# A transformer layer on one core: V from gathered columns in all nine units, one PSUM tile for each part of the last pair, and new engine orders

## The chip, the core and the metric

The kernel runs on one core of a Trainium2 chip. The core has five engines that run side by side, each through its own list of instructions: TensorE (PE, matrix products; its weight loads are shown as PEld), VectorE (DVE), ScalarE (ACT), GpSimd (POOL) and SyncE (SP), which here only issues DMAs. ScalarE issues some DMAs too. Engines wait for each other through semaphores. The metric is the device time of one execution in microseconds, the median of several runs.

## The reference

The input x has 2048 rows (tokens) of 448 numbers in bf16. A small vector c gives six modulation vectors. The layer has an attention half and a feed-forward half:

```python
mod = silu(c) @ w_mod                      # 6 x 448: sa, ca, ga, sb, cb, gb
h = layernorm(x) * (1 + ca) + sa
qkv = h @ wqkv                             # 16 heads of 28
# token s attends to tokens s, s-2, s-4, ..., s-14 (8 keys, where they exist)
logits = q . k * 28 ** -0.5
o = softmax(logits) @ v
x = x + ga * (o @ wo)
h = layernorm(x) * (1 + cb) + sb
x = x + gb * (silu(h @ w1) @ w2)           # hidden size 1792
```

Since keys lie two tokens apart, even and odd tokens never meet in the attention.

## The kernel before

**Tiles.** The 2048 tokens are split by parity into two series of 1024. A *pair* m (0 to 7) is 128 positions of both parities, 256 tokens, two tiles of 128 rows. A *chunk* k (0 to 3) is two pairs. The normalised and modulated activations lie transposed, features on the partitions, in two tiles `hA` and `hB` of 512 positions each (shown as ha and hb), as [feature, parity, block, position]. The 448 features lie in four blocks of 128, so that a product over 448 is seven matmuls of 64 rows. Two of these, on the upper and lower 64 rows, run side by side. Each such product is two operations: S, four steps on equal halves, and C, three steps on crossed halves (function `pair`). C starts only after S has ended, so other work is put between them.

**Stages.** For every chunk: statistics (L361, L362), `rstd` on GpSimd (L374, L375), the shift `nm` on VectorE or GpSimd (L381, L383, L385), the normalised `xn` on ScalarE (L393) or VectorE (L395). The first chunk is transposed by TensorE (L455) and modulated out of PSUM in blocks (`modp`, L234 on ScalarE, L236 on VectorE); the other chunks are transposed by DMA (L412) and modulated in place (`mod`). The Q and K weights are copied to a padded tile `wp` (`pad`, L441). Then come the Q and K products (L483), evicted at L487.

**Attention units.** Queries are handled in nine units u of two blocks of 57 positions, each block with its 64 keys. `project_v(u)` computes V for a unit's keys, both blocks and both parities. A key block of 64 positions starts anywhere, and its two parities lie 512 columns apart or more, so there are two ways to feed it as stationary operand. *Apart*: two matmuls of 64 rows by 64 columns, one for each parity, four running side by side, 28 in all (L518). *Whole*: the columns are first copied (`gather`, L507) to a tile `hv`, where both parities lie next to each other, and then 14 matmuls of 64 by 128 do it (L517). A set says which units are apart; all but unit 4 are, whose keys lie across hA and hB. After V come logits (L555), exp on ScalarE (L562), the mask (L613), the weighted sum of V (L629), reciprocal and scaling (L636, L641), a transpose by DMA (L644), the copy to its place (`align`, L651 to L659), and the output projection (L686) with the residual (L694).

**Feed-forward.** For each chunk: 14 column blocks of w1 in seven products (L714), silu on ScalarE (L719), and for each pair the product with w2 (L741), an addition of x on VectorE (`ya`, L774) and a store (`sto`, L779). The last pair, m = 7, is done in pieces so that its end is short: `full` (L753) computes F0 and F1 (rows of parity 0), F2 (parity 1, first 224 columns) and F3 (parity 1, last 224 columns), with three additions ya70, ya71, ya72 and three stores (L781). All four write one PSUM tile.

**Order.** Each of the 578 operations has a number and an engine; `ORDER` lists them, and `Plan.emit` issues them in that order, so that it is every engine's program. The letter behind a number chooses the engine (p TensorE, a ScalarE, v VectorE, g GpSimd, s SyncE). There are four PSUM tiles of two banks; an operation with `take=("ps",)` takes the next free one, and `P.release` says which operation gives it back. Where two engines write overlapping parts of a tile, the framework adds a wait for the one issued first. TensorE fills its first microseconds with products of zeros (`warm_up`, L297): "warm" is 12 matmuls, and each "junk" two; a junk given to SyncE is nothing. Should a sum of exponentials fall out of range, the layer runs again in a safe form (L891); this doesn't happen with these inputs.

## Time and profile before

| | us |
|---|---|
| median of 3 runs | 170.31 |
| lowest, highest | 169.68, 170.35 |
| the profiled execution | 169.34 |
| its span, first to last instruction | 167.5 |
| TensorE busy | 156.1 |
| ScalarE busy | 102.0 |
| VectorE busy | 86.1 |
| GpSimd busy | 25.5 |

A row of the profile in order of time has the start in us from the span's start, the length in us, the engine (SPq and ACTq: a DMA being issued), the line of the kernel, the operation, out<-in by tile names, the shape, and how many instructions were merged; in brackets stands the engine's idle time before it and what ended it. A row of the grouped view has the line, engine, operation, tiles and count, then busy us, mean ns of one, and idle us before. A row of DMA issues has tiles, issuing queue, count, size, and us from issue to landing. Matmuls overlap, so the length of one (349 or 376 ns) is longer than the distance from one to the next; a stretch of many is read from the start of its first to the start of what follows.

### The profile page before, as it was taken

Reading aid. Unit: us, or ns where it says so; the run is one execution under the profiler, and the core shown is the slowest. Engines: PE = TensorE matmul, PEld = TensorE weight load, DVE = VectorE, ACT = ScalarE, POOL = GpSimd, SP = SyncE. Lnnn points to the kernel's source line nnn. Section 1 sums busy time; section 2 is a strip of 40 time slices with the busy share of each in tenths; the row PEclk is TensorE's granted clock in tenths of the full one; section 3 lists DMA queues with packets and bytes.
Section 4 is the critical chain, followed back from the end, with each engine's and each line's share of the span. In section 5 each row is a group of like instructions: output and inputs, shape, how many; then the busy total and the mean of one; then the engine's idle time right before and its main releaser. Section 6 shows DMA issues by size and latency. Waiting matters only on the chain. (4 is left out here: it accounts for less than half of the span.)

```text
span 167.5 us, 6069 instructions
## 1 busy us (share of the span) xinstructions
PE 156.1 (93%) x2670; PEld 80.5 (48%) x2670; DVE 86.1 (51%) x192; ACT 102.0 (61%) x138; POOL 25.5 (15%) x66
## 2 busy tenths in 40 slices
PE   2979979999999999999999999999999999999950
PEld 1254535655455555444556444454444444445540
DVE  3897899987888747692668713302152002002220
ACT  4368657879866869997976695894266620440000
POOL 7460730700002200312034000022000000000000
PEclk9999999999999999999999999999999999999996
DMA  5989978658640999920220950002411000000412
GB/s 138 348 293 242 247 289 135 180 101 171 162 126 21 198 174 293 250 56 7 59 66 22 121 125 4 0 0 57 126 55 55 4 0 4 0 0 4 170 32 87
DMA packets 33453, 18.52 MB, mean 111 GB/s; under 512 B 25102, under 2 KB 33422, under 8 KB 33422
## 3 DMA queue, kind: packets, MB, share of 16 engines
q1 hardware_dynamic: 30208, 14.46, 37.6%
q10 hardware_dynamic: 3214, 3.61, 6.9%
q8 instruction: 23, 0.38, 0.9%
q14 instruction: 8, 0.07, 0.1%
HBM read 10.21 MB, written 1.84 MB: 72 GB/s over the span
## 5 line engine op out<-in xcount | busy, mean ns | idle before, releaser
L719 ACT ACTIVATE both<-ps 128x1024 bf16<-128x1024 f32 x28 | 27.8, 1021 | 23.6 <-PE ps L714 23.6
L741 PE MATMUL ps<-w,both 64*128 64x448 bf16 x392 | 39.9, 349 | 0.0
L714 PEld LDWEIGHTS <-w 64*128 64x128 bf16 x392 | 19.0, 94 | 21.9
L741 PEld LDWEIGHTS <-both 64*128 64x128 bf16 x392 | 18.8, 94 | 18.2
L714 PE MATMUL ps<-wqk,w 64*128 64x512 bf16 x196 | 23.3, 376 | 0.0
L714 PE MATMUL ps<-h,w 64*128 64x512 bf16 x196 | 23.1, 376 | 0.0
L562 ACT ACTIVATE p<-ps 128x912 bf16<-128x912 f32 x18 | 15.8, 928 | 5.7 <-PE ps L555 5.6
L483 PEld LDWEIGHTS <-wp 64*128 64x128 bf16 x224 | 11.0, 94 | 13.4 <-issue 3.2
L694 DVE SCALAR_TENSOR_TENSOR x_all<-ps,x_all 128x448 bf16<-128x448 f32 x16 | 9.3, 621 | 15.0 <-PE ps L686 15.0
L483 PE MATMUL ps<-ha,wp 64*128 64x512 bf16 x112 | 13.2, 377 | 1.1 <-DVE ha L236 1.1
L483 PE MATMUL ps<-hb,wp 64*128 64x512 bf16 x112 | 14.0, 377 | 0.0
L487 ACT CAST qk<-ps 128x1024 bf16<-128x1024 f32 x11 | 11.0, 1016 | 4.0 <-PE ps L483 4.0
L374 POOL TENSOR_SCALAR rs<-mv 128x2 f32<-128x2 f32 x16 | 3.9, 242 | 61.3 <-ACT scr L371 45.6
L393 ACT ACTIVATE xn<-x_all,nm,rs 128x512 bf16<-128x512 bf16 x12 | 9.1, 806 | 6.2 <-DVE nm L381 5.7
L613 DVE TENSOR_TENSOR p<-p,maskb 128x1824 bf16<-128x1824 bf16 x9 | 10.1, 1118 | 4.4 <-ACT p L562 4.4
L774 DVE TENSOR_TENSOR wqk<-ps,x_all 128x896 bf16<-128x896 f32 x4 | 4.4, 1089 | 15.5 <-PE ps L741 13.4
L375 POOL TENSOR_TENSOR rs<-rs,negh 128x2 f32<-128x2 f32 x16 | 11.8, 740 | 1.3
L774 DVE TENSOR_TENSOR ot<-ps,x_all 128x896 bf16<-128x896 f32 x3 | 3.3, 1091 | 16.1 <-PE ps L741 16.1
L361 DVE BATCH_NORM_STATS2 st<-x_all 128x6 f32<-128x448 bf16 x16 | 9.7, 605 | 3.3 <-DMA x_all<-in_A_x_dram 3.3
L395 DVE TENSOR_SCALAR xn<-x_all,mv,rs 128x512 bf16<-128x512 bf16 x20 | 7.3, 402 | 6.9 <-POOL rs L375 6.5
L371 ACT ACTIVATE scr<-x_all,mv 128x448 bf16<-128x448 bf16 x16 | 10.6, 665 | 0.1
L641 DVE TENSOR_TENSOR o<-ps,rc 121x896 bf16<-121x896 f32 x9 | 9.7, 1078 | 0.2
(96 smaller groups left out, 170.8 us busy)
## 6 DMA issues: line engine op xcount, KB each, us to landing
both<-in_w_mod_dram SPq DMA_DIRECT2D x3, 672.0 KB, 6.0
w<-in_B_w_dram SPq DMA_DIRECT2D x3, 448.0 KB, 4.4
x_all<-in_A_x_dram ACTq DMA_DIRECT2D x2, 448.0 KB, 4.7
out_dram<-wqk SPq DMA_DIRECT2D x4, 224.0 KB, 2.0
w<-in_B_w_dram ACTq DMA_DIRECT2D x1, 784.0 KB, 6.1
w<-in_B_w_dram SPq DMA_DIRECT2D x1, 784.0 KB, 5.7
both<-in_w_mod_dram SPq DMA_DIRECT2D x3, 224.0 KB, 5.1
wo<-in_A_wo_dram ACTq DMA_DIRECT2D x1, 672.0 KB, 5.0
```

Source lines behind the costliest of these rows:

```text
L361: V.bn_stats(out=st[:], in_=x_all[:, us[t], :])
L371: S.activation(out=scr[:, t, :], in_=x_all[:, us[t], :], func=ACTF.Square, bias=mv[:, t, 0:1], accum_out=mv[:, t, 1:2])
L375: G.tensor_tensor(out=rs[:], in0=rs[:], in1=negh[:], op=ALU.pow)
L483: return [matmul(t[:, j, :], lhsT=w, rhs=hT[k // 2][rows, :, kt, CP * (k % 2):CP * (k % 2) + CP], start=start, stop=stop)]
L487: copy_on(o)(out=qk[:, :, g, :, s0:s0 + CP], in_=t[:].rearrange("p j (t s) -> p j t s", t=2))
L562: S.activation(out=p_of[u][:, 2 * t * w:2 * t * w + 2 * w].rearrange("p (j n) -> p j n", j=2), in_=bank(a, t)[:, :, 0:w], func=ACTF.Exp, s ...
L613: V.tensor_tensor(out=p, in0=p, in1=m, op=ALU.mult)
L641: V.tensor_tensor(out=dims(t[0:n, :], 0, (576, 2), (DH, H), (1, DH)), in0=view(bank(a))[:, :, :, 0:DH], in1=r, op=ALU.mult)
L694: V.scalar_tensor_tensor(out=x_all[:, u, :], in0=ps[first["slot"]["ps"][0]][:, par, 0:D], scalar=1.0, in1=x_all[:, u, :], op0=ALU.mult, op ...
L714: return [matmul(t[:, i // 7, :], lhsT=w1[rows, kt, 128 * i:128 * i + 128], rhs=h[rows, :, kt, :], start=start, stop=stop)]
L719: S.activation(out=hid[:, k % 2, :, i, :], in_=t[:], func=ACTF.Silu)
L741: x = matmul(t[:, par, 0:D], lhsT=hid[half(hf), k % 2, jj, ii, 128 * j:128 * j + 128], rhs=w2[half(hf), ii + 7 * jj, :], start=(way == 0 a ...
```

## The change

Three things change.

1. `APART` becomes empty: all nine V units are "whole". Eight more gathers are issued, and 8 x 28 matmuls of 64x64 become 8 x 14 of 64x128. A gather reads the modulated activations of all pairs that hold its keys.
2. The last pair takes three PSUM tiles: one for F0 and F1, one for F2, one for F3. Each addition reads its own, and each tile is given back by its own addition.
3. `ORDER` is another list, of 586 operations. Its numbers are not comparable with the old ones, since the eight gathers shift them. By name, the parts of it that differ at the start and the end are these (junks on SyncE left out):

| engine | before, start | after, start |
|---|---|---|
| SyncE | ldx0a ldx0b ldm_a1 ldx1 ldm_a0 ldwv0 ldwqk0, n13.tr n12.tr, ldm_b0 ldm_c0 ldm_c1 ldm_b1, n14.tr ldwo1 n15.tr | ldx0a ldc ldx0b ldx1 ldm_a0 ldwqk1 ldwqk0 ldwv0 ldwv1, n13.tr ldm_c1 n12.tr, ldm_b0 ldw21 ldwo0, n15.tr ldm_b1 n14.tr |
| GpSimd | vone3 rcone masks, rstd of n10, n11, n13, vone2, n13.nm, n12.rstd, vone1, n12.nm, vone0, rstd of n15, n14, ones ozero0 ozero1 | ozero1 vone3 masks vone2 vone1 ones, n10.rstd n10.nm n11.rstd n11.nm n12.rstd n13.rstd n13.nm n14.rstd vone0 rcone n15.rstd n15.nm ozero0 |
| ScalarE | ldc tab silu_c scT, n10.xn0 ldwv1 n10.xn1 n11.xn0 ldwqk1 n11.xn1, h00.mod1, ldx2 ldx3, n13.xn0 n13.xn1, pad2, v0.ev v1.ev qk02.ev qk03.ev | tab ldm_a1 silu_c, n10.xn0 scT n10.xn1 ldx2 n11.xn0 n11.xn1 ldx3, h00.mod1 h01.mod0, n12.xn0 n12.xn1, hv0 hv1, qk01.ev qk00.ev qk03.ev |
| VectorE | statistics and shifts of the first four tiles, mod1.ev, h00.mod0 h01.mod0 h01.mod1, pad0, n12.xn0 n12.xn1 screp, pad3 pad1 | statistics of the first four tiles, mod1.ev, pad2 pad3, h00.mod0 h01.mod1, pad0 pad1, n12.nm n13.xn0 n13.xn1 |
| TensorE | ccol warm, 6 junks, mod1.mm h00.trp h01.trp, v0.S v1.S v0.C v1.C, qk03 and qk02, qk01 and qk00, qk11 and qk10 with lg0 between | ccol warm, 3 junks, mod1.mm h00.trp h01.trp, 5 junks, qk00 and qk01, qk02 and qk03, v1.S v0.S lg0 v0.C v1.C, qk10.S qk13.S lg1 |

Here n1m is pair m's normalisation (st, rstd, nm, xn, tr), ldx the loads of x, ldm those of w_mod, ldwqk, ldwv, ldwo, ldw1, ldw2 those of the weights, hv a gather, ozero and vone and rcone and ones memsets of constant parts, `.ev` an eviction. At the end, before: F0 F1 F2 F3, then ya6, ya70, sto70 (SyncE), ya71, sto71 (SyncE), sto6 (SyncE), ya72, sto72 (ScalarE). After: ya6, sto6 (SyncE), F0 F1 F2, ya70, sto70 (ScalarE), ya71, sto71 (ScalarE), F3, ya72, sto72 (SyncE). Between these, every engine's list is another, too: the gathers of units 0, 1, 2 and 5 are on ScalarE, the others on VectorE.

```diff
-APART = (0, 1, 2, 3, 5, 6, 7, 8)
+APART = ()
...
 ORDER = """
-2a 25a 58a 59p 60a 0s 30g 33g 68v 69v 1s 26g 70g 74v 75v 76g 71v 4s 35p 54p 72a 6a 73a 39p 51s 37p 44p 42p 50p 40s 41s 9s 52s 53s 43s 3s 111v 110v
...
-374s 514s 562p 563p 564p 567p 568p 569p 570p 571p 565v 572v 573s 574v 575s 566s 576v 577a
+32g 0s 68v 30g 25a 26g 4a 69v 2s 58a 59p 29g 28g 34g 35p 57p 39p 45s 46p 70g 71g 72a 60a 73a 42s 1s 75v 74v 76g 77g 9s 3s 52s 8s 7s 62p 106v 107v 10a
...
+557a 510p 511p 567p 568p 569p 512p 570p 513v 514s 522s 571p 572p 573v 574s 575p 576p 577p 578p 580v 581a 582v 583a 579p 584v 585s
 """
...
             if last_pair:
-                def full(o, par, i0, i1, c0, c1, i=i, cell=cell):
-                    t = ps[cell["first"]["slot"]["ps"][0]]
+                def full(o, par, i0, i1, c0, c1, i=i, mms=mms):
+                    t = ps[mms[2 * par + (c0 > 0)]["slot"]["ps"][0]][:, 0, 0:c1 - c0]
                     for ii in range(i0, i1):
                         for jj in range(2):
-                            matmul(t[:, par, c0:c1], lhsT=hid[:, k % 2, jj, ii, 128 * (2 * i + par):128 * (2 * i + par) + 128], rhs=w2[:, ii + 7 * jj, c0:c1],
+                            matmul(t, lhsT=hid[:, k % 2, jj, ii, 128 * (2 * i + par):128 * (2 * i + par) + 128], rhs=w2[:, ii + 7 * jj, c0:c1],
                                    start=(ii == 0 and jj == 0), stop=(ii == 6 and jj == 1))
...
-                                  take=() if x else ("ps",), group=("F", None, 0))
+                                  take=() if x == 1 else ("ps",), group=("F", None, 0))
...
-                V.tensor_tensor(out=t[:, p, c0:c1], in0=ps[cell["first"]["slot"]["ps"][0]][:, p, c0:c1], in1=x_all[:, 2 * m + p.start:2 * m + p.stop, c0:c1], op=ALU.add)
+                r = ps[(mms[2 * par + (c0 > 0)] if last_pair else cell["first"])["slot"]["ps"][0]]
+                r = r[:, p, :][:, :, c0:c1] if par is None else r[:, 0:1, 0:c1 - c0]
+                V.tensor_tensor(out=t[:, p, c0:c1], in0=r, in1=x_all[:, 2 * m + p.start:2 * m + p.stop, c0:c1], op=ALU.add)
...
-            P.release(ad, first, "ps")
-            if not last_pair:
+            P.release(ad[:1], first, "ps")
+            if last_pair:
+                for x in (1, 2):
+                    P.release(ad[x:x + 1], mms[x + 1], "ps")
+            else:
                 P.release(st, ad[0], "out")
```

## The prediction

> **What bounds the kernel now.** I read the page first, then TensorE alone in order of time, then the other engines in the two stretches where TensorE waits: the first 22 us and the last 6.

> ```profile
> span 167.5 us, 6069 instructions
> PE 156.1 (93%) x2670; PEld 80.5 (48%) x2670; DVE 86.1 (51%) x192; ACT 102.0 (61%) x138; POOL 25.5 (15%) x66
> PE   2979979999999999999999999999999999999950
> ```

> The profiled execution took 169.34 us, of which 167.5 are the span and 1.84 lie around it. TensorE is full in every slice but the first few and the last two. So a change counts in three ways only: when the unbroken stream of matmuls starts, how much work is in it, and what follows its end. TensorE in order of time:

> ```profile
> 3.22 5.03 PE L297 MATMUL ps<-junk 64*128 64x512 bf16 x24
> 8.90 0.95 PE L322 MATMUL ps<-scT,both 128*128 128x1 bf16 x32 [0.65 <-DMA both<-in_w_mod_dram]
> 9.71 1.05 PE L455 MATMUL ps<-ident,xn 128*128 128x128 bf16 x16
> 10.83 0.70 PE L518 MATMUL ps<-wv,ha 64*64 64x448 bf16 x8
> 11.80 2.73 PE L518 MATMUL ps<-wv,ha 64*64 64x448 bf16 x48 [0.27 <-ACT ha L234]
> 14.47 6.54 PE L483 MATMUL ps<-ha,wp 64*128 64x512 bf16 x58
> 21.36 0.39 PE L483 MATMUL ps<-ha,wp 64*128 64x512 bf16 x2 [0.36 <-DVE ha L236]
> 22.45 1.47 PE L483 MATMUL ps<-ha,wp 64*128 64x512 bf16 x12 [0.70 <-DVE ha L236]
> ...
> 31.20 1.52 PE L518 MATMUL ps<-wv,ha 64*64 64x448 bf16 x28
> 32.55 0.70 PE L629 MATMUL ps<-v,p 64*57 64x29 bf16 x64
> ...
> 39.33 0.94 PE L517 MATMUL ps<-wv,hv 64*128 64x448 bf16 x8
> 40.20 0.70 PE L555 MATMUL ps<-qk 28*64 28x57 bf16 x64
> 40.83 0.74 PE L517 MATMUL ps<-wv,hv 64*128 64x448 bf16 x6
> ```

> The stream begins with V of units 0 and 1 (L518), ragged until 11.80 because the activations arrive piece by piece. The first Q/K product (L483) starts at 14.47. It stands still for 0.36 and 0.70 us at 21 to 22.45, and from there nothing stops it until the last product.

> **The tail.** The rows after the last product (L753):

> ```profile
> 155.75 5.51 PE L753 MATMUL ps<-w,both 128*128 128x448 bf16 x42
> 156.47 1.09 DVE L774 TENSOR_TENSOR wqk<-ps,x_all 128x896 bf16<-128x896 f32 x1 [2.06 <-DMA out_dram<-wqk]
> 161.36 1.22 DVE L774 TENSOR_TENSOR qk<-ps,x_all 128x448 bf16<-128x448 f32 x3 [3.80 <-PEq L891]
> 162.01 1.17 SPq L781 DMA_DIRECT2D out_dram<-qk  x2
> 162.61 0.38 ACTq L781 DMA_DIRECT2D out_dram<-qk  x1
> 163.24 0.42 SPq L779 DMA_DIRECT2D out_dram<-wqk  x1
> ```

> ```profile
> out_dram<-wqk SPq DMA_DIRECT2D x1, 224.0 KB, 2.4
> out_dram<-qk SPq DMA_DIRECT2D x1, 56.0 KB, 2.0
> L774 DVE TENSOR_TENSOR qk<-ps,x_all 128x224 bf16<-128x224 f32 x2 | 0.7, 379 | 0.0
> ```

> All three additions of the last pair run after the last matmul (155.75 + 5.51 = 161.26), although the first has had its sum for some 3 us: all four groups write one PSUM tile. Then SyncE issues two of the three stores and, only behind them, the store of pair 6, whose addition was done at 157.56. That store lands last, at 163.24 + 2.4 = 165.64, and 1.86 us later the span ends. So 6.24 us follow the last matmul.

> After the change, addition one and two each wait for their own PSUM tile and fall under the matmuls that remain; their stores go to ScalarE's queue, where nothing else waits. Pair 6's store goes out ahead of the last one on SyncE. What is left behind the last matmul is 0.10 (161.36 - 161.26) + 0.38 for one addition of 224 columns + 0.03 to the issue (162.61 after the addition's end at 162.58) + 2.0 landing + 1.86 = 4.37 us. Gain 6.24 - 4.37 = **1.87 us**. Bounds: 1.0 if the additions still wait for the last matmul (161.26 + 0.10 + 1.22 + 0.03 + 2.0 + 1.86 = 166.47 against 167.5), 2.3 if a quarter of the final 1.86 us runs beside the landing. Covers: 2.8 us of matmuls hide the first addition's 0.63, some 1.2 the second's 0.38.

> **The V units.** 28 matmuls of 64x64 occupy TensorE from 31.20 to 32.55: 1.35 us. The 14 gathered ones of 64x128 take 0.87 (39.33 to 40.20) and up to 0.74, 1.6 at most, but in two pieces with other shapes of matmul between, which the 1.35 hasn't.  I take nothing for TensorE; bounds -0.4 (shared shapes saved elsewhere) to +0.8 for eight units (0.1 us each, 0.05 a piece). The eight added gathers are two copies of 128x512 each, four on VectorE and four on ScalarE (unit 4's was on VectorE already):

> ```profile
> L507 DVE COPY hv<-ha 128x504 bf16<-128x504 bf16 x1 | 0.3, 287 | 0.0
> L651 ACT COPY oa<-op 128x448 bf16<-128x448 bf16 x1 | 0.6, 564 | 0.9 <-DMA op<-o 0.9
> ```

> That is 0.6 us a unit on VectorE and 1.2 on ScalarE, some 2.3 and 4.8 us in all, on engines busy 51 and 61% of the span. They hide under TensorE's stream as long as no eviction queued behind them is late; the first, on ScalarE ahead of the first Q/K evictions, have 6 us of Q/K products over them.

> **The start.** Gathered V needs all of the first chunk and its copies, so now Q/K goes first, and it cannot begin on a part: it needs both pairs' eight modulated blocks and all four padded weights. The rows that time this:

> ```profile
> 6.51 0.81 ACT L393 ACTIVATE xn<-x_all,nm,rs 128x512 bf16<-128x512 bf16 x1 [3.02 <-DVE nm L381]
> 9.40 0.80 ACT L393 ACTIVATE xn<-x_all,nm,rs 128x512 bf16<-128x512 bf16 x1
> 11.19 0.56 ACT L234 ACTIVATE ha<-ps,modc 128x256 bf16<-128x256 bf16 x1 [0.98 <-DVE ha L236]
> 11.65 0.56 ACT L234 ACTIVATE ha<-ps,modc 128x256 bf16<-128x256 bf16 x1
> ...
> 10.36 2.00 DVE L236 TENSOR_SCALAR ha<-ps,modc 128x256 bf16<-128x256 bf16 x6
> 13.56 0.69 DVE L441 COPY wp<-wqk 128x896 bf16<-128x896 bf16 x2
> 19.82 2.58 DVE L236 TENSOR_SCALAR ha<-ha,modc 128x512 bf16<-128x512 bf16 x3
> ...
> 4.12 0.29 POOL L279 TENSOR_SCALAR_AFFINE_SELECT maskb<-maskb 64x114 bf16<-64x114 bf16 x1
> 5.16 0.19 POOL L374 TENSOR_SCALAR rs<-mv 128x2 f32<-128x2 f32 x1 [0.75 <-DVE mv L362]
> 10.05 0.22 POOL L385 TENSOR_SCALAR nm<-nm 128x2 f32<-128x2 f32 x1
> 19.40 0.10 POOL L286 MEMSET onesf<- 128x1 f32 x1
> 19.99 2.26 POOL L283 MEMSET o<- 128x1088 bf16 x2
> ```

> GpSimd first. Its masks ended at 4.41 and the first rstd began at 5.16, when its statistics came. Now one memset of ob (half of 2.26: 1.13), two more V memsets (0.35) and the ones (19.40 to 19.99: 0.6) stand ahead of it, and rc's memset (0.3) moves away: it begins at about 4.41 + 1.8 = 6.2, 1.0 late. The shift nm, formerly VectorE's, follows on GpSimd, 0.5. So ScalarE's first normalisation begins at about 7.6 instead of 6.51. The other three follow at 0.8 each, with scT between, and end near 10.9 instead of 10.20. The second pair's eight transposes (half of 1.05) end near 11.5.

> VectorE: padding two, 0.7; pair 0's two blocks at 0.33 (2.00 / 6) to 11.7; pair 1's two to 12.4; padding two more to 13.1. The half of the Q and K weights that the old order loaded last was padded at 13.56; now some 0.9 MB fewer stand ahead of it in the queues (V's weights and the other half), so I take both halves as early enough. ScalarE's blocks each wait for VectorE's of the same pair, as at 11.19; two take 1.02 us, so four run from 11.75 to 13.7. TensorE can take up its first pair of matmuls near 13.2 and is free near 13.7: I take **13.5**.

> In the old order, V0 and V1 back to back would be 14 groups at 0.19 (1.35 / 7), 2.65 us, so the stream effectively began at 14.47 - 2.65 = 11.8. Slip **+1.7**; bounds +0.8 (GpSimd's list costs nothing) and +2.5 (weights or clock a microsecond later).

> Against it stand the two stalls, 0.36 + 0.70 = **-1.06**. They came from VectorE's three blocks of 19.82, 2.58 us for what takes 1.1 elsewhere, while GpSimd ran its two memsets of 19.99. In the new order one memset is done at the start, and the second chunk's blocks are needed only near 23.3: 13.5 + 28 pairs at 0.225 (6.54 / 29) + 2 x 1.4 for V0 and V1 + 0.70 for a unit's logits. [...]

> Later in the stream, third-chunk blocks have hardly any slack in the new order: VectorE's list puts pair 4's normalisation behind the masks of units 0 and 1. I add **+0.3** for new stalls; bounds 0 and 1.5.

> **Sum.** 169.34 - 1.87 + 1.7 - 1.06 + 0 + 0.3 = 168.4 in a profiled execution. The median of the runs is 170.31, 0.97 above the profiled one, so I predict **169.3 us**, 0.6% less. About 0.5%, 0.85 us, is what a measurement of this kernel can tell from no change.

> **The rivals.**

> *The start slips little.* If GpSimd's list fits ahead of the statistics, the slip is 0.8 and no new stall comes: 169.3 - 0.9 - 0.3 = 168.1. For it: TensorE's five fillers behind the transposes fill only 5 x 0.23 = 1.1 us, too little for 2 us. Against: the memsets' durations above. Chance 0.20.

> *A slow clock, slower than before.*

> ```profile
> L297 PE MATMUL ps<-junk x24: 377/627/631, 3.2 to 7.9; 64*128 64x512 bf16 x24
> ```

> The fillers run at 0.42 us a pair (5.03 / 12); only the last, at 7.9, has the 377 ns of the later products, which go at 0.225 a pair (6.54 / 29). So 4.65 us of work passed before TensorE was fast. The new order has 9 pairs there, 3.8 us, and idles before and after the transposes. If that never opens the clock, the Q/K products pay: 4.65 x (1 - 0.225 / 0.42) = 2.15 us, hence 171.4. It decides if the Q/K matmuls from 13.5 on go at 0.42 a pair. Against it: the fast pace also survived a gap of 0.65 us at 8.25. [...] Chance 0.20.

> *Stalls take the place of those removed.* The third chunk's blocks or an eviction behind a gather hold TensorE for 1.5 instead of 0.3: 170.5. For it: the copies' 2.3 and 4.8 us fall in the busiest part of both engines' lists. Against: the old order, with lists nearly as long, has no gap after 22.45. Chance 0.13.

> *The additions still wait.* Then only pair 6's store gains: 169.3 + 0.87 = 170.2. Chance 0.05.

> **How the numbers follow.** My forecast keeps 0.42, with its own range 168.6 to 170.0: two thirds of it below 169.46. Faster: 0.28 + 0.20 = 0.48. Same: 0.14 of mine, 0.05, 0.08 of the stalls, 0.03 of the clock = 0.30. Slower: 0.17 of the clock, 0.05 of the stalls = 0.22. The range reaches from 167.2 (early start with the larger tail gain) to 171.4 (the slow clock).

> **What would show it.** In the changed profile: the first addition of qk before the last L753 ends, and about 4.4 us from the last matmul to the span's end; L483's first matmul near 13.5 with GpSimd's first rstd near 6.2; no idle time at L483 from ha near 21 us; L517 taking 1.35 to 1.6 us a unit; L483's pace 0.225 a pair from the first. I am wrong if Q/K starts before 12.5 or after 14.5, if its pace is 0.42, or if TensorE idles over 1 us after 23.

## The result: 3.2% slower, and the profile after

The changed kernel takes 176.7 us (174.96 to 177.97 in 4 runs) against 170.33 us (169.68 to 171.48) for the kernel before. The ratio is 1.0323, with a 95% interval from 1.0257 to 1.039. I had predicted 169.3 us and a range up to 171.4. The time lies above the range, on the other side of no change. Some executions of one kernel take a few per cent longer than its others; ratios and intervals here leave out those over 1.5% above the fastest, medians do not, and the profiles of after_apart, before_whole and shift_split below are of such longer ones.

The profiled execution took 174.96 us. TensorE is busy for 157.1 us of it, against 156.1 before. From the page of the changed kernel, the span, TensorE's slices, and the queue that brings program code:

```profile
span 173.2 us, 5865 instructions
PE   0879949999897999999999999999999999999990
q8 instruction: 22, 0.36, 0.9%
```

A slice is 4.33 us. The 4 in the sixth (7 before), the 8 in the eleventh and the 7 in the thirteenth (9 before) are new. TensorE in order of time, start, length, line and count, with the idle time before a row and its releaser in brackets:

```profile
13.22 6.46 PE L483 MATMUL ps<-ha,wp 64*128 64x512 bf16 x56 [0.95 <-ACT ha L234]
...
21.76 0.55 PE L517 MATMUL ps<-wv,hv 64*128 64x448 bf16 x4
24.57 1.68 PE L517 MATMUL ps<-wv,hv 64*128 64x448 bf16 x8 [2.26 <-issue]
26.01 2.89 PE L483 MATMUL ps<-ha,wp 64*128 64x512 bf16 x16
28.83 0.70 PE L555 MATMUL ps<-qk 28*64 28x57 bf16 x64
...
34.62 1.49 PE L517 MATMUL ps<-wv,hv 64*128 64x448 bf16 x14
35.94 0.38 PE L483 MATMUL ps<-ha,wp 64*128 64x512 bf16 x2
...
46.38 0.44 PE L629 MATMUL ps<-v,p 64*57 64x29 bf16 x35
47.89 0.40 PE L629 MATMUL ps<-v,p 64*57 64x29 bf16 x29 [1.06 <-issue]
...
51.69 0.74 PE L686 MATMUL ps<-wo,oa 64*128 64x448 bf16 x5
53.71 0.36 PE L686 MATMUL ps<-wo,oa 64*128 64x448 bf16 x1 [1.28 <-issue]
53.83 1.96 PE L483 MATMUL ps<-hb,wp 64*128 64x512 bf16 x16
55.72 0.70 PE L555 MATMUL ps<-qk 28*64 28x57 bf16 x64
...
59.22 1.02 PE L629 MATMUL ps<-v,p 64*57 64x29 bf16 x103 [0.32 <-issue]
...
163.17 5.51 PE L753 MATMUL ps<-w,both 128*128 128x448 bf16 x42
```

Four stops of 2.26, 1.06, 1.28 and 0.32 us, 4.92 in all, were not there before. They do not fall between operations: the weighted sum of one unit (L629, 64 matmuls) is cut into 35 and 29. "issue" means that the profile shows nothing that the engine waited for, no semaphore, eviction or load. After the longest one TensorE is slow as well. The same profile in stretches, with TensorE's busy time and count first and the granted clock after the five engines:

```profile
22.00:24.57 2.57, 0.31 (x5) 0.05 (x2) 0.40 (x2) 0.96 (x2) 1.31 (x3) 1.00 1.09 374
24.57:28.00 3.43, 3.43 (x18) 1.60 (x19) 1.65 (x4) 1.74 (x2) 0.00 (x0) 0.50 0.62 171
```

The clock is 0.50 for 3.43 us. In it the 8 matmuls of 24.57 took 1.44 us, where 14 of the same kind took 1.32 at 34.62 (so 0.75 for 8), and the 16 of 26.01 took 2.82 against 1.89 at 53.83: 0.69 + 0.93 = 1.6 us lost.

The end of the last matmul moved from 161.26 to 163.17 + 5.51 = 168.68, 7.42 us. The start of Q/K accounts for 13.22 - 11.8 = 1.42 of it, the two stalls that are gone for -1.06. So 7.06 us are new stops and slowness; 4.92 + 1.6 = 6.5 of them are in these rows, and the other 0.5 I did not place.

The tail, all engines together:

```profile
166.10 0.62 DVE L776 TENSOR_TENSOR qk<-ps,x_all 128x448 bf16<-128x448 f32 x1 [1.67 <-PE ps L753]
...
168.71 0.39 DVE L776 TENSOR_TENSOR qk<-ps,x_all 128x224 bf16<-128x224 f32 x1 [0.88 <-PE ps L753]
```

The first addition begins 2.58 us before the last matmul ends, and 173.2 - 168.68 = 4.5 us follow it, instead of 6.24.

### The profile page after: what moved, and what is told of

Its sections match the earlier page's. It is cut to its first block, busy times and chain, and to the rows that moved or that the text cites. A ratio compares the mean times of both kernels' runs of the same rounds, so it can differ in the third digit from the quotient of the medians.

```text
span 173.2 us, 5865 instructions
## 1 busy us (share of the span) xinstructions
PE 157.1 (91%) x2562; PEld 81.2 (47%) x2562; DVE 89.3 (52%) x205; ACT 100.1 (58%) x139; POOL 24.0 (14%) x70
## 2 busy tenths in 40 slices
DMA packets 33452, 18.50 MB, mean 107 GB/s; under 512 B 25102, under 2 KB 33422, under 8 KB 33422
## 3 DMA queue, kind: packets, MB, share of 16 engines
HBM read 10.21 MB, written 1.84 MB: 70 GB/s over the span
## 4 chain that ended last, share of the span: by engine, by line
PE 80%; DVE 8%; DMA 5%; issue 3%; ACT 1%; SPq 0%; DVEq 0%
PE ps L714 25%; PE ps L741 21%; PE ps L483 15%; PE ps L686 5%; PE ps L517 5%; PE ps L753 3%; DMA w<-in_B_w_dram 3%; PE ps L629 3%; PE ps L555 3%; DVE st L361 2%; DMA x_all<-in_A_x_dram 2%; DVE mv L362 1%; DVE qk L487 1%; DVE ha L236 1%; DVE o L641 1%
## 5 line engine op out<-in xcount | busy, mean ns | idle before, releaser
L741 PE MATMUL ps<-w,both 64*128 64x448 bf16 x392 | 38.7, 349 | 0.0
L714 PEld LDWEIGHTS <-w 64*128 64x128 bf16 x392 | 18.8, 94 | 22.3 <-DMA w<-in_B_w_dram 0.5
L714 PE MATMUL ps<-wqk,w 64*128 64x512 bf16 x196 | 22.8, 376 | 0.0
L776 DVE TENSOR_TENSOR ot<-ps,x_all 128x896 bf16<-128x896 f32 x4 | 4.4, 1092 | 31.8 <-ACT both L719 17.5
L483 PEld LDWEIGHTS <-wp 64*128 64x128 bf16 x224 | 12.0, 97 | 13.4 <-issue 2.8
L517 PE MATMUL ps<-wv,hv 64*128 64x448 bf16 x126 | 15.0, 364 | 2.3 <-issue 2.3
L694 DVE SCALAR_TENSOR_TENSOR x_all<-ps,x_all 128x448 bf16<-128x448 f32 x16 | 9.6, 621 | 13.2 <-PE ps L686 8.5
L483 PE MATMUL ps<-ha,wp 64*128 64x512 bf16 x112 | 14.3, 397 | 1.0 <-ACT ha L234 0.9
L374 POOL TENSOR_SCALAR rs<-mv 128x2 f32<-128x2 f32 x16 | 3.6, 224 | 77.6 <-ACT scr L371 70.9
L483 PE MATMUL ps<-hb,wp 64*128 64x512 bf16 x112 | 13.4, 376 | 0.1
L393 ACT ACTIVATE xn<-x_all,nm,rs 128x512 bf16<-128x512 bf16 x13 | 10.2, 810 | 5.1 <-POOL nm L385 3.0
L517 PEld LDWEIGHTS <-hv 64*128 64x128 bf16 x126 | 6.4, 96 | 7.8 <-issue 2.7
## 6 DMA issues: line engine op xcount, KB each, us to landing
out_dram<-ot SPq DMA_DIRECT2D x4, 224.0 KB, 2.1
```

The costliest lines, as they stand in the source:

```text
L393: S.activation(out=out_, in_=in_, func=ACTF.Identity, scale=rs[:, t:t + 1], bias=nm[:, t:t + 1])
L483: return [matmul(t[:, j, :], lhsT=w, rhs=hT[k // 2][rows, :, kt, CP * (k % 2):CP * (k % 2) + CP], start=start, stop=stop)]
L517: return [matmul(t[:, j, 0:D], lhsT=w, rhs=wv[rows, kt, :], start=start, stop=stop)]
L714: return [matmul(t[:, i // 7, :], lhsT=w1[rows, kt, 128 * i:128 * i + 128], rhs=h[rows, :, kt, :], start=start, stop=stop)]
L741: x = matmul(t[:, par, 0:D], lhsT=hid[half(hf), k % 2, jj, ii, 128 * j:128 * j + 128], rhs=w2[half(hf), ii + 7 * jj, :], start=(way == 0 a ...
```

## What the stops are: TensorE's own program arrives late

```
kernel        number  asked   packet from-to   ran out  went on  went on - packet's end
after            449  14.97   22.29 - 23.22     21.96    24.57    1.35
after           1473  42.42   45.40 - 46.36     46.65    47.88    1.52
after           1729  47.88   50.96 - 52.40     52.08    53.70    1.30
after           1985  53.70   56.95 - 57.83     58.72    59.22    1.39
before           449  12.48   14.04 - 14.97     no stop (needed at 23.92)
before           705  23.92   24.75 - 25.85     no stop (needed at 28.10)
before          2753  58.35   60.43 - 61.36     no stop (needed at 62.88)
```

Where the packet ended 1.4 us or more ahead of its use, as everywhere in the kernel before, there is no stop of this size; where it ended later, TensorE goes on some 1.4 us after its end. With the k-th packet put to the k-th of these numbers, the same comes out in all the runs: 18 stops of over 0.3 us lie at such numbers, and TensorE went on 1.30 to 1.52 us after the end of the packet in each.

Why was the first one late? The DMA engines of the changed kernel from 15 to 25 us, busy tenths and queue share:

```profile
DMA  9994293799999973388999999999999999999997
q1 hardware_dynamic: 4205, 2.86, 98.9%
```

2.86 MB of loads and transposes pass in these 10 us, and from 14.97 to 22.29 the DMA engines are busy for 98%. The packet starts only then. In a window of 22.25 to 22.35 us its start shows as the one slot of 7629 GB/s (slot 15 of 40, 22.29):

```profile
GB/s 717 358 0 0 358 0 717 0 717 358 717 0 0 1075 7629 0 358 0 0 358 0 717 358 358 358 717 0 0 1075 358 717 0 358 0 358 0 717 0 717 0
```

Before, in a window of 13.9 to 15.2 us, the same packet starts in slot 5 of 40 (945 GB/s), at 14.04, three us before the four loads of w_mod that SyncE issues from 17.0 on:

```profile
GB/s 552 221 496 276 945 276 441 386 386 386 165 551 276 441 276 496 276 496 221 441 386 331 496 221 496 276 441 221 441 166 331 276 221 331 55 292 63 292 252 284
```

The packet does not simply stand in a line, though. SyncE issued the three largest of the loads at 16.94, 17.57 and 18.11, after 14.97, and from 18.50 to 19.25 the engines were busy for only 49% without the packet starting. In the kernel before they were busy for 92% from 12.48 to 14.04, mostly with ScalarE's loads of x, and the packet still started within 1.56 us. And for the later stops the loads explain less. While TensorE's packet for number 1729 was on its way (47.88 to 50.96), the DMA engines moved nothing at all (the last two numbers of the row are their busy share and GB/s):

```profile
47.90:50.90 3.00, 3.00 (x57) 1.57 (x57) 2.96 (x7) 1.35 (x2) 0.00 (x0) 1.00 0.00 0
```

The kernel before has the same at number 3521: 3.8 us (76.42 to 80.23) with nothing else moving, harmless there because the code was needed only at 83.1. So that late code stops TensorE is one statement, and that loads make it late is another, which needs its own experiments.

My theory at this point: the new order lets bulk loads stand ahead of TensorE's code, and puts operations with many short matmuls next to each other, so that a block is used up faster than the next one comes. The rivals were the gathers, a plain data wait, and a tail that did not work.

## The experiments

**tail_alone.** The kernel before, with only the three PSUM tiles and the order of the tail; V and the start as before.

```diff
-374s 514s 562p 563p 564p 567p 568p 569p 570p 571p 565v 572v 573s 574v 575s 566s 576v 577a
+374s 514s 562p 563p 564p 565v 566s 567p 568p 569p 570p 572v 573a 574v 575a 571p 576v 577s
...
-                                  take=() if x else ("ps",), group=("F", None, 0))
+                                  take=() if x == 1 else ("ps",), group=("F", None, 0))
```

> The kernel before with only the last pair changed: three PSUM tiles, additions and stores in the new order, pair 6's store ahead of the last product; all nine V units and the rest of the order as before. My theory of the tail: the first two additions run under the last matmuls, about 4.4 to 4.6 us follow the last matmul instead of 6.24, and the time falls by 1.7 us to 168.6 (ratio 0.990). Rival (the tail is hidden anyway, or the additions still wait): within 0.5 us of before.

Measured: 169.11 us against 170.54, ratio 0.9914 (0.9879 to 0.9949). The last matmuls and the first addition of its last pair:

```profile
156.77 4.93 PE L753 MATMUL ps<-w,both 128*128 128x448 bf16 x39
159.12 0.62 DVE L776 TENSOR_TENSOR qk<-ps,x_all 128x448 bf16<-128x448 f32 x1 [1.11 <-PE ps L753]
```

The addition begins 2.6 us before the last matmul ends (161.70), and 4.4 us of the span of 166.1 follow that end. The tail is worth 1.5 us here (0.0086 x 170.5), with an interval of 0.9 to 2.1. The predicted 1.87 lies inside, and the loss comes from elsewhere.

**late_loads.** The changed kernel, with the loads of 784 and 672 KB for the second w2 half and wo taken from SyncE's list and issued by ScalarE, at 27.96 and 24.73 instead of 17.57 and 18.11 us.

```diff
-SyncE:   n13.tr ldm_c1 n12.tr ldm_b0 ldw21 ldwo0 n15.tr ldm_b1
+SyncE:   n13.tr ldm_c1 n12.tr ldm_b0 n15.tr ldm_b1
-ScalarE: ... ldm_c0 ex01 ... ldwo1 hv2
+ScalarE: ... ldm_c0 ldwo0 ex01 ... ldwo1 ldw21 hv2
```

> The changed kernel, but the two large loads w2 second half (784 KB) and wo (672 KB), which SyncE issued at 17.6 and 18.1 us, go to ScalarE's queue some 8 to 12 us later. Theory A (TensorE ran out of instructions: the fetch of its next 16 KB of code waits behind the loads): the fetch seen at 22.3 us comes before 21, the gap of 2.26 us at L517 near 22 shrinks below 0.8 us, the half clock after it (24.6 to 28.0) disappears, the gaps of 1.1, 1.3 and 0.4 us at 46 to 59 stay; time 4 us below the changed kernel, 172 to 173.5. Rival B (the matmuls wait for the gathers or for a PSUM tile): the gap stays, time 175 to 178.

Measured: 173.35 us, ratio 1.018 (1.0116 to 1.0243). TensorE in order of time:

```profile
22.93 0.55 PE L517 MATMUL ps<-wv,hv 64*128 64x448 bf16 x4
23.90 0.93 PE L517 MATMUL ps<-wv,hv 64*128 64x448 bf16 x8 [0.42 <-issue]
24.66 1.91 PE L483 MATMUL ps<-ha,wp 64*128 64x512 bf16 x16
...
40.62 3.63 PE L483 MATMUL ps<-hb,wp 64*128 64x512 bf16 x32 [1.98 <-ACT gbc L343]
```

The stop stands at the same matmul of the same V product and shrinks from 2.26 to 0.42 us. Only a part of this is the loads' doing: the packet starts at 21.54 instead of 22.29, 0.75 us earlier and not before 21 as I had expected, and TensorE itself comes to the place 1.17 us later (23.13 instead of 21.96), for it had a slow start in this execution, with the clock at 0.50 from 11.96 to 15.37. The 16 Q/K matmuls behind the stop take 1.83 us instead of 2.82: with the shorter stop the slow clock there is gone. I had expected the later stops to stay, but those at 1473 and 1729 are gone as well, and 0.32 us is left at 1985. Some of the gain goes again at 40.62, where a product waits for ScalarE's `gbc`. ScalarE was late with it because it had waited 2.89 us for a transpose (hb<-xn), issued at 33.01 and landed at 39.25; the delayed load of w2 landed only at 35.38.

**after_apart.** The changed kernel's order and tail, without the gathers: V apart in eight units, as before.

```diff
-APART = ()
+APART = (0, 1, 2, 3, 5, 6, 7, 8)
...
 # ORDER: the changed one without the eight gathers
```

> The changed kernel's order and tail, but eight V units from 64x64 matmuls on the ungathered activations again, the eight gathers left out of the order. Theory A (late code, set by the order of loads and by how fast instructions are used up): the gap near 22 us stays at 1.5 us or more, the time stays above 173. Rival B (gathers or gathered V cost the time): the gaps go, the time falls to 169 to 171.

Measured: 176.34 us (172.14 to 180.3; before 170.54). Three executions took 175.95 us or more, one 172.14, too far apart for a ratio, so only the place of the stops is read, in the execution of 175.95:

```profile
21.99 0.61 PE L555 MATMUL ps<-qk 28*64 28x57 bf16 x53
25.93 0.25 PE L555 MATMUL ps<-qk 28*64 28x57 bf16 x11 [3.33 <-issue]
```

The program is another, so number 449 is now in the logits, after 53 of 64 matmuls. There it stops for 3.33 us, and goes on 1.34 us after the end of its packet at 24.59. Further stops lie at 1985 and 2241. So such stops need no gathers. In the execution of 172.14 the granted clock was 1.00 throughout, against 0.99 in this one, so there no slow time can have followed a stop; how long its stops were is not known.

**shift_code and shift_timed.** One kernel, in a single execution and then in ten: the changed one with eight more fillers in the first 13 us, 32 instructions on TensorE. Nothing else moves, but each block of 256 now ends 32 instructions earlier in the real work.

```diff
-... 57p 39p 45s 46p 70g ... 42s ... 52s ... 50p 49p 82a ... 37s 47s ... 53s ... 40s 36s
+... 57p 39p 46p 37p 52p 42p 45p 70g ... 50p 49p 36p 40p 53p 47p 82a
```

> The changed kernel with eight fillers more on TensorE (16 products of zeros and 16 weight loads, in its idle time before 13.2 us), so that every later operation stands 32 instructions further back in TensorE's program. Theory A: the gaps come at the same counts of instructions, 449, 1473, 1729 and 1985 executed, whatever operation stands there: the first moves from V (L517) into the first unit's logits (L555), the third from the output projection (L686) into unit 4's logits (L555). Rival B (a wait of the operation itself): the gaps stay at L517 and L686. Time about as the changed kernel.

> The changed kernel with eight fillers more, as before (32 instructions earlier in TensorE's program), now timed against the kernel before. Theory A: the fetch at instruction 193 is asked for before the loads of 15 us and comes by 14.5, no gap at instruction 449, no half clock; gaps only at 705 or 2241, 2 us in all; 169.0 to 171.0, ratio 0.99 to 1.005. Rival B (the one look at this kernel was luck): back to 174 to 178.

Measured: 169.82 us in the single execution, then 170.74 us against 170.18, ratio 1.0014 (0.9979 to 1.0048). Eight fillers take 6 us off. In shift_timed's window of 13.2 to 14.4 us the packet for number 449 starts in slot 3 of 40 (905 GB/s), at 13.27:

```profile
GB/s 329 358 905 299 359 239 299 299 239 299 179 179 299 60 239 119 239 120 60 179 0 239 0 60 120 0 60 0 60 0 0 60 0 60 0 60 0 0 60 0
```

The instruction 256 earlier ran at 12.77 instead of 14.97, since fillers and not Q/K products had used up those before it, and the packet starts ahead of everything that SyncE issues from 13.60 on. TensorE of shift_timed:

```profile
21.78 1.31 PE L517 MATMUL ps<-wv,hv 64*128 64x448 bf16 x12
23.04 1.90 PE L483 MATMUL ps<-ha,wp 64*128 64x512 bf16 x16
...
53.65 0.59 PE L483 MATMUL ps<-hb,wp 64*128 64x512 bf16 x3
55.33 2.33 PE L483 MATMUL ps<-hb,wp 64*128 64x512 bf16 x19 [1.09 <-issue]
```

No stop near 22 us, no slow clock. My expectation for shift_code was half wrong: the rule of the places held, with stops of 0.65 and 0.83 us at 705 and 2241, but none of the four stops that I had named came, and I had expected the time of the changed kernel. What is left in shift_timed is a stop in front of number 2241 = 449 + 7 x 256, after 53.65. There the loads play no part, for the DMA engines moved nothing between 51.96 and 53.02: the 256 instructions were used up in 1.90 us (51.96 to 53.86), because the weighted sums of units 3 and 4 stand next to each other, and the packet (53.02 to 53.91) came 1.06 us after the earliest moment that the table would give it. A further 0.94 us is lost in front of 2753, whose packet started at 65.79, while loads ran.

The level with the kernel before is not the work of the code packets alone. The runs of shift_timed had a granted clock of 0.993 to 1.00, those of the kernel before beside them 0.972 to 0.992. Whether the fillers are the cause of that, and how much it is worth, was not measured. The gain over the changed kernel is not of this kind, for in that one's profiled execution the clock is up from 7.53 to 24.60.

**shift_split.** The same, with the second of these weighted sums moved behind the Q/K product that follows, and its two VectorE steps moved back.

```diff
-TensorE: wo1.S av3 av4 wo1.C qk30.S qk33.S qk30.C v5.S
+TensorE: wo1.S av3 wo1.C qk30.S qk33.S qk30.C av4 v5.S
-VectorE: ... on3 ... rc4 on4 n20.xn0 n20.xn1 qk33.ev n21.nm
+VectorE: ... on3 ... n20.xn0 n20.xn1 qk33.ev rc4 on4 n21.nm
```

> Edit: the kernel with the eight more fillers (shift_timed, 170.74 us), with the weighted sum of unit 4 (128 instructions) moved from directly behind that of unit 3 to behind the Q/K product qk30, some 1.4 us of longer matmuls later, and its two VectorE steps moved back with it. Theory (TensorE's code arrives late): in shift_timed the 256 instructions up to number 2241 were used up in 1.90 us (51.96 to 53.86) and TensorE then stood until 55.32. Spread out, the same 256 last 3 us or more, their successor's transfer of about 1 us ends in time, and the stop at 2241 shrinks from 1.46 to 0.4 us or less; the time falls by 0.6 to 1.3 us, to 169.3 to 170.2, ratio to before 0.993 to 0.999. A stop can come up at 2497 or 2753, whose blocks arrive behind loads, up to 1 us. Rival (the stop belongs to the Q/K product qk33 itself, by an eviction or a free PSUM tile that is late): it stays in front of that product, 1.0 to 1.5 us, wherever the weighted sum stands, and the time stays at 170.7.

Measured: 172.59 us against 170.34, ratio 1.0075 (1.0023 to 1.0128). The gain that I expected (0.993 to 0.999) did not come; a loss against shift_timed is not shown, for the two intervals overlap. TensorE, SyncE (with shift_timed's two rows behind the dots) and ScalarE, in an execution of 173.62 us:

```profile
53.65 2.54 PE L483 MATMUL ps<-hb,wp 64*128 64x512 bf16 x22
...
71.61 5.10 PE L714 MATMUL ps<-h,w 64*128 64x512 bf16 x30 [2.51 <-ACT v L523]
```

```profile
61.06 1.24 SPq L644 DMA_TRANSPOSE op<-o  x1
62.34 3.64 SPq L412 DMA_TRANSPOSE h<-xn  x2
...
56.91 1.24 SPq L644 DMA_TRANSPOSE op<-o  x1
58.20 4.03 SPq L412 DMA_TRANSPOSE h<-xn  x2
```

```profile
69.95 0.81 ACT L234 ACTIVATE h<-h,modc 128x512 bf16<-128x512 bf16 x1 [5.23 <-DMA h<-xn]
```

The stop at 2241 is gone: the 22 matmuls from 53.65 on run in one piece. That part of the theory held, and the rival, which tied the stop to the product, fell. In this execution the time was lost elsewhere. I had moved VectorE's steps of unit 4 by some 4 us, and SyncE's transpose of that unit waits for them: it is issued at 61.06, against 56.91 in shift_timed, and behind it in SyncE's list the transposes of the next stage at 62.34 against 58.20. ScalarE then waits 5.23 us for them, and an eviction queued behind holds TensorE for 2.51 us, after which the clock is 0.50 from 72.40 to 75.81. I had asked only what the moved matmuls do, not what stands behind them in a third engine's list.

**before_bulk.** The other way round: the kernel before, with the two large loads put ahead of SyncE's last w_mod load, as in the new order.

```diff
-SyncE:   ... ldm_b0 ldm_c0 ldm_c1 ldm_b1 ... ldw21 ...
+SyncE:   ... ldm_b0 ldm_c0 ldm_c1 ldw21 ldwo0 ldm_b1 ...
-ScalarE: ... ex10 ldwo0 ex11 ...
+ScalarE: ... ex10 ex11 ...
```

> The kernel before with only two loads moved: w2 second half (784 KB) and wo (672 KB) go out on SyncE right behind the loads of w_mod near 19 us, as in the changed kernel. Theory A: the loads then last until 28 us instead of 24.7, the fetch that came at 24.75 comes near 28, and TensorE stands still at instruction 705 (28.1 us) for 1 to 2.5 us, all at once, with the gathers, V and engine orders of before; 171.5 to 174. Rival B (loads don't hold up the fetch): no gap at 705, within 0.7 us of before.

Measured: 173.83 us, ratio 1.02 (1.0136 to 1.0264). TensorE:

```profile
29.60 0.59 PE L555 MATMUL ps<-qk 28*64 28x57 bf16 x51
31.51 0.26 PE L555 MATMUL ps<-qk 28*64 28x57 bf16 x13 [1.32 <-issue]
...
34.47 1.32 PE L518 MATMUL ps<-wv,ha 64*64 64x448 bf16 x21
37.36 0.57 PE L518 MATMUL ps<-wv,ha 64*64 64x448 bf16 x7 [1.57 <-issue]
```

The stops come in front of numbers 705 and 961. The instructions 256 earlier ran at 25.80 and 31.51, and the packets started at 29.17 and 34.92, 3.4 us later each, where the kernel before has 0.84 and 1.29. So the old kernel, too, stops when bulk loads are set ahead, with nothing else changed. In the profiled execution (175.06 us) the two stops make 1.32 + 1.57 = 2.9 us. A good part of the rest is a later start, number 193 running at 14.96 instead of 12.48: TensorE waited 3.40 us for a load of w_mod, up to 10.68, where the kernel before waited 0.65, and the clock was 0.50 from 9.30 to 16.13. The two moved loads are issued only at 21.26 and 22.02, so this part is not their work. After these shorter stops the clock stayed at 1.00.

**before_whole.** The kernel before, with the eight gathers, each put right ahead of its use.

```diff
-APART = (0, 1, 2, 3, 5, 6, 7, 8)
+APART = ()
...
-ORDER: ... ldwv0 v0.S ... n12.xn0 v1.S ...
+ORDER: ... ldwv0 hv0 v0.S ... n12.xn0 hv1 v1.S ...
```

> The kernel before, its order and tail, with all nine V units from gathered columns: eight gathers put in right ahead of their unit, units 0, 3 and 6 on ScalarE, the others on VectorE. Theory A: gathering by itself costs only the later start of V0 and V1 (0.8 to 2 us) and some waits for gathers that this order didn't plan; no gap above 0.5 us except at instructions 449 + 256 n; 170.5 to 173. Rival B (gathered V is what costs): 175 or more.

Measured: 184.42 us, ratio 1.0754 (1.0665 to 1.0843), far above what I expected. TensorE, and the granted clock after the first of its stops:

```profile
13.59 5.63 PE L517 MATMUL ps<-wv,hv 64*128 64x448 bf16 x28 [2.22 <-ACT hv L507]
...
34.71 0.36 PE L517 MATMUL ps<-wv,hv 64*128 64x448 bf16 x1 [1.88 <-ACT hv L507]
```

```profile
12.00:18.80 6.80, 5.21 (x27) 2.01 (x29) 6.53 (x21) 4.64 (x8) 1.32 (x6) 0.50 0.75 213
```

The gathers come late, four times by 1.7 to 2.2 us, and beside or behind three of these waits the clock is 0.50: from 12.00 to 18.80, from 35.90 to 39.20 and from 59.80 to 63.10. I had put 175 or more down for the rival that gathered V is what costs; here it is the waits for gathers in this order, and the slow clock with them. So this run doesn't price a gather that is issued in time, which was its purpose. It does show that "whole" V needs an order in which the copies run well ahead, which the changed order has.

**tail_and_memsets.** tail_alone, with the two memsets of `o` moved from the end of GpSimd's opening list to between its second and third rstd.

```diff
-GpSimd: ... n14.rstd ones ozero0 ozero1
+GpSimd: ... n11.rstd ozero0 ozero1 n13.rstd ... n14.rstd ones
```

> The kernel before with the new tail, and GpSimd's two memsets of ob moved from 20 us to between the rstd of pairs 1 and 3. If these memsets are what stretched VectorE's three blocks and stopped TensorE at 21 to 22.5 us: no idle time at L483 from ha, 1.0 us less than the tail alone, 167.5 to 168.5, ratio 0.985. If the blocks are slow for another reason: as the tail alone, 168.6 to 169.3.

Measured: 168.28 us against 170.18, ratio 0.9895 (0.9816 to 0.9974), the fastest of all. GpSimd's memsets, TensorE's Q/K products and VectorE's three blocks:

```profile
7.46 1.95 POOL L283 MEMSET o<- 128x1088 bf16 x2
```

```profile
15.62 7.94 PE L483 MATMUL ps<-ha,wp 64*128 64x512 bf16 x72
```

```profile
20.66 1.05 DVE L236 TENSOR_SCALAR ha<-ha,modc 128x512 bf16<-128x512 bf16 x3
```

With the memsets away, the three blocks take 1.05 us instead of 2.58: that the stretch came from the memsets is shown by this. The Q/K products, 72 matmuls, run in one piece, but that is not shown to come from it. In tail_alone's profile the memsets still run at 20.00, the blocks still take 2.58 us, and the 72 matmuls run in one piece as well, from 16.00 on: they began 1.5 us later than in the kernel before, and the blocks were in time. So the 0.36 and 0.70 us are lost only where Q/K starts early. How much the move is worth on top of the tail is not shown either, for the two ratios overlap.

## Why the prediction was wrong, step by step

**The start: right in its parts.** GpSimd and ScalarE of the changed kernel:

```profile
5.88 0.19 POOL L374 TENSOR_SCALAR rs<-mv 128x2 f32<-128x2 f32 x1
```

```profile
7.47 0.81 ACT L393 ACTIVATE xn<-x_all,nm,rs 128x512 bf16<-128x512 bf16 x1 [2.99 <-POOL nm L385]
...
11.69 1.93 ACT L234 ACTIVATE ha<-ps,modc 128x256 bf16<-128x256 bf16 x4 [1.06 <-DVE ha L236]
```

First rstd at 5.88 (6.2 predicted), first normalisation 7.47 (7.6), the modulated blocks from 11.69 (11.75), Q/K from 13.22 (13.5). The slip was 1.42 instead of 1.7.

**The two stalls at 21 us: right.** The 56 Q/K matmuls from 13.22 on run in one piece.

**V: right.** 14 matmuls in one stretch take 35.94 - 34.62 = 1.32 us, against 1.35 for 28 before. Nothing was gained on TensorE, and after_apart stops without a gather too.

**The tail: right.** 4.5 us after the last matmul, 4.37 predicted; alone it makes the kernel 0.9% faster.

**"I add +0.3 for new stalls; bounds 0 and 1.5": this step failed.** It was 7.06 us. I looked for stalls only where a list's order could make data late, and the third-chunk blocks that I feared were in time. What came was a wait of a kind that the trace of before does not hold, because there each code packet came in time by 1.4 us or more. The page of before did show the queue (23 packets of instructions), and I passed over it. A price can be set on the first stop, as an estimate afterwards: the 2.4 MB of loads that the new order sets together from 14.97 on, at the 288 GB/s that the engines moved on average over 15 to 25 us, take 8.3 us; a packet that waited for all of them would start at 23.3, and with its 0.94 us and the 1.4 behind it TensorE would go on at 25.6, 3.6 us after it ran out. It was 2.6. So the bound of 1.5 was too low for this stop alone. For the stops at 1473 to 1985 no such price follows, since at 1729 nothing moved.

**The rivals.** "Stalls take the place of those removed" named the right kind with the wrong cause and a fifth of the size. "A slow clock" came, but not at the start of the profiled execution: there the clock was up from 7.53 to 24.60, and it dropped to 0.50 after the first stop, which cost 1.6 us. The other two did not come: the start slipped by 1.42, and the additions no longer waited.

**From the profile to the median.** My sum for the profiled execution was 168.4, and it took 174.96: 6.6 us, made of about 6.8 for the stops, -0.3 for the start and +0.15 for the tail. The other 0.8 of the 7.4 us between 169.3 and 176.7 is that the median now lies 1.7 us above the profiled execution, where I had carried over 0.97. That difference is no fixed amount. The profiled execution of the kernel before had its clock up from 7.84 on (0.992 over the span), while 12 of the 13 executions beside tail_alone had 0.977 to 0.986. tail_alone, with the same start, shows what that can mean: TensorE waited 1.10 us for w_mod instead of 0.65, the clock was 0.50 from 11.45 to 14.86, and Q/K began at 16.00 instead of 14.47. So the start from which I counted was one of the good ones. One slip of the working changes nothing in the outcome: the low end of the range, an early start with the larger tail gain, is 168.1 - (2.3 - 1.87) = 167.7, not 167.2.

What stays open is the worth of whole V in an order where code comes in time. shift_timed, with all of the change and little stopping, is level with the kernel before (1.0014), though its tail alone gives 0.9%; it still stops for 1.09 and 0.94 us. How these divide among the start, V and the stops was not taken apart further. Nor does any run show why the first block ends at number 449 and not at a multiple of 256, or what holds a packet back by 3 us and more: SyncE's loads do it in before_bulk, but which transfers do it in the changed kernel, loads or transposes, and what does it where nothing moves, stays open.

## What to carry to other kernels

In these runs a stop put down to "issue" in the middle of one operation was a mark of late program code: 18 stops of over 0.3 us stood at number 449 or a multiple of 256 behind it. So count the engine's instructions to such a stop, and look for even steps between the stops. When loads are moved forward or set together, look at the instruction queue of the page as at any other transfer: with two loads set ahead, two packets started 3.4 us after the instruction 256 earlier instead of 0.84 and 1.29 (before_bulk), and where operations of many short instructions (128 in 0.65 us) stood next to each other, 256 were used up in 1.90 us and TensorE stopped for 1.09 (shift_timed). And a step moved on one engine moves whatever stands behind its consumer in a third engine's list.

## What the runs showed of the hardware that I had not expected

Eight fillers, 3.4% in time: the same work went from 176.7 to 170.74 us when the borders of the code blocks fell elsewhere, early enough for the first packet to start at 13.27 instead of 22.29, ahead of the loads. From a late packet's end to the moment when TensorE runs on, 1.30 to 1.52 us passed in each of the stops in the table.

In the changed kernel's trace the granted clock rises at 7.53, falls to 0.50 at 24.60 and rises at 28.01, which are 5 x 3.41 and 6 x 3.41 us after 7.53. The other times at 0.50 whose start and end were read last as long or twice as long: 11.96 to 15.37 in late_loads, 11.45 to 14.86 in tail_alone, 72.40 to 75.81 in shift_split, 9.30 to 16.13 in before_bulk. After the first 20 us, the clock was 0.50 behind TensorE's stops of 2.26 us (the changed kernel), 3.33 (after_apart, in the window of 27.20 to 30.50), 2.51 (shift_split), and 1.88 and 1.97 (before_whole); it stayed at 1.00 behind those of 1.06 and 1.28 (the changed kernel) and 1.32 and 1.57 (before_bulk). Behind late_loads' stop of 1.98 us, too, the 32 Q/K matmuls from 40.62 on took 3.63 us, 0.227 a pair and so the fast pace; why this one cost no clock was not shown. An estimate: if steps of 3.41 us run on from 8.54, where late_loads' clock first rose, one ends at 39.26 (8.54 + 9 x 3.41), inside that stop, and leaves 0.62 us of it on one side and 1.36 on the other. In the first 12 us a shorter wait was followed by the slow clock as well: 1.10 us in tail_alone. The stop of 2.26 us cost 1.6 us more by the slow clock.
